# Gated linear attention feeding a softplus feed-forward layer: first four blocks loaded in pairs with two tokens per partition, loads strictly in turn, headwise score products, bias sum late

## The chip, the cores and the metric

The kernel runs on one core of one Trainium2 chip. The metric is the device time of one execution, in microseconds (us). A run of the unchanged kernel stands beside every run of a variant on the same chip. The kernel before takes 199.03 us (median of 3 runs, 198.89 to 200.34). A run is called slow when it is over 1.5% above the fastest run of the same kernel; comparisons use fast runs alone.

Five engines work side by side: TensorE (PE in the profile), VectorE (DVE), ScalarE (ACT), GpSimd (POOL) and SyncE (SP), which here issues all DMA transfers.

## The reference

```python
def _attn_ref(q, k, v, f_logit):          # each (4, 8, 768, 48)
    f = 1.0 / (1.0 + np.exp(-f_logit))
    state = np.zeros((B, H, D, D), dtype=np.float32)
    for t in range(S):
        state = f[:, :, t, :, None] * state + einsum('bhd,bhe->bhde', k[:, :, t], v[:, :, t])
        y[:, :, t] = einsum('bhd,bhde->bhe', q[:, :, t], state)
    return y
def _moe_ref(x, w_in, w_out):             # x (3072, 384), w_in (384, 2048), w_out (2048, 384)
    h = x @ w_in
    g = np.maximum(h, 0.0) + np.log1p(np.exp(-np.abs(h)))
    return g @ w_out
```

`x` is the attention output with the 8 heads of 48 side by side. The kernel works in 24 blocks of 128 tokens (4 batches of 6). In a block the running product of the gates becomes a prefix sum of logarithms, the in-block part a masked product of scores, and the earlier part a 48 x 48 state per head.

## The kernel before

A static list decides, ahead of time and from estimated costs, in which order each engine receives its tasks. A task names its engine, its cost, what it needs, a priority, and the buffers it takes and frees. So a change in one buffer count or cost can reorder every engine.

The loads: one 192 KB transfer for each of f, k, q and v of a block, in rows of one token of one head (48 floats, 192 bytes). The first four blocks go ahead of the eight weight quarters.

```python
def load(n, i):
    b, c = divmod(i, NC)
    t = work.tile([128, H, D], FP32, name=n + n, tag=n + n, bufs=LOADS)
    nc.sync.dma_start(
        out=t, in_=SRC[n][b, :, c * T:(c + 1) * T, :].rearrange("h p d -> p h d"))
    in_t[n, i] = t
# ... cut
turn = TURN or (blocks(0, 1, 2, 3) + [("wi", w) for w in range(4)]
                + [("wo", w) for w in range(4)])
```

The score products of blocks 4 to 23 take two heads at once, through a block-diagonal copy of q that costs VectorE two copies of 48 rows:

```python
def a_bd(i):
    pv, qbd = qkT_ps[i, 0], qbd_bufs[i % 2]
    nc.vector.tensor_copy(out=qbd[0:48, :, 0:128], in_=pv[0:48])
    nc.vector.tensor_copy(out=qbd[64:112, :, 128:256], in_=pv[64:112])
def a_p(i, half):                       # two calls of two matmuls for a block
    ps = att_bank("pp")
    for u in range(2):
        p = 2 * half + u
        nc.tensor.matmul(out=ps[:, u * 256:(u + 1) * 256], lhsT=qkT_t[i][0:112, NP + p, :],
                         rhs=qbd_bufs[i % 2][0:112, p, :], start=True, stop=True,
                         skip_group_check=True)
```

The softplus is computed as ln(0.5 e^h + 0.5), so the missing ln 2 comes back as a bias on the output, ln 2 times the column sums of w_out. GpSimd makes it with 15 additions, `sum`, from the staged weights; blocks finished earlier get it later through `add`:

```python
for n, (w, j) in enumerate(sums):
    task(("sum", n), "POOL", 0.91, [("at", "wo", w), ("sum", n - 1)], 40 + 3 * n, add_w, (w, j))
# ... cut
def store(i):
    nc.sync.dma_start(out=out[i * T:(i + 1) * T, :], in_=osb_t.pop(i))
    if i in (19, 20, 21):               # loads that nothing reads
        m = 2 << (i - 19)
        t = consts.tile([96, H, m, D], FP32, name=f"rows{m}")
        nc.sync.dma_start(out=t, in_=q[0, :, 0:96 * m, :].rearrange("h (p m) d -> p h m d", m=m))
```

The feed-forward layer is `f1` (48 matmuls of 128 columns for a block), two activations, and `f2` (16 matmuls of 384 columns).

## Time and profile before

| | before |
|---|---|
| time, median | 199.03 us |
| span of the profiled run | 197.0 us |
| first feed-forward matmul starts | 24.72 us |
| holes of TensorE after that | 6.7 us |
| last matmul starts, then the tail | 193.31 us, 3.66 us |
| VectorE, GpSimd busy | 142.9, 98.1 us |

The span is from the first to the last instruction of one profiled execution. A matmul's useful time is the distance from its start to the next start, capped at the median of its line; what exceeds that is a **hole**. Matmuls of fewer rows than the array are kept apart, with the excess ahead of their group (entry) and behind it (exit).

The page of the kernel before says, in its busy row and in the shares of the chain that ended last:

```profile
PE 184.4 (94%) x2491; PEld 152.7 (78%) x2491; DVE 142.9 (73%) x336; ACT 150.1 (76%) x251; POOL 98.1 (50%) x142
...
PE 57%; DVE 12%; SPq 10%; POOL 8%; DMA 6%; ACT 3%; issue 2%; ACTq 0%; POOLq 0%
```

The first line alone would say that TensorE is full at 94%, but 13.9 us of that are matmuls that only keep the clock up. In the chain TensorE has 57%; for the rest of the span the chain runs through other engines and transfers.

### The profile page before, as it was taken

Reading aid. Unit: us, or ns where it says so; the run is one execution under the profiler, and the core shown is the slowest. Engines: PE = TensorE matmul, PEld = TensorE weight load, DVE = VectorE, ACT = ScalarE, POOL = GpSimd, SP = SyncE. Lnnn points to the kernel's source line nnn. Section 1 sums busy time; section 2 is a strip of 40 time slices with the busy share of each in tenths; the row PEclk is TensorE's granted clock in tenths of the full one; section 3 lists DMA queues with packets and bytes.
Section 4 is the critical chain, followed back from the end, with each engine's and each line's share of the span. In section 5 each row is a group of like instructions: output and inputs, shape, how many; then the busy total and the mean of one; then the engine's idle time right before and its main releaser. Section 6 shows DMA issues by size and latency. Waiting matters only on the chain.

```text
span 197.0 us, 6209 instructions
## 1 busy us (share of the span) xinstructions
PE 184.4 (94%) x2491; PEld 152.7 (78%) x2491; DVE 142.9 (73%) x336; ACT 150.1 (76%) x251; POOL 98.1 (50%) x142
## 2 busy tenths in 40 slices
PE   6886997899999999989999999999999999999993
PEld 5775786666687888868888888888888888888872
DVE  6543774625999989999989889858778988773011
ACT  4566388886859996987989797898879778766770
POOL 2266867999997652652463364344246334500000
PEclk9999999999999999999999999999999999999998
DMA  6999999999999999999978757846541101102676
GB/s 124 188 189 176 352 382 374 244 198 187 188 165 194 186 190 173 277 195 208 233 146 172 144 118 160 161 113 137 113 90 41 42 2 43 40 29 75 163 188 171
DMA packets 109532, 32.34 MB, mean 164 GB/s; under 512 B 101184, under 2 KB 107968, under 8 KB 109504
## 3 DMA queue, kind: packets, MB, share of 16 engines
q1 hardware_dynamic: 109504, 31.96, 78.4%
q8 instruction: 19, 0.31, 0.7%
q14 instruction: 9, 0.07, 0.1%
HBM read 27.23 MB, written 4.72 MB: 162 GB/s over the span
## 4 chain that ended last, share of the span: by engine, by line
PE 57%; DVE 12%; SPq 10%; POOL 8%; DMA 6%; ACT 3%; issue 2%; ACTq 0%; POOLq 0%
PE hh L407 22%; PE ops L427 21%; SPq L140 8%; DMA w<-in_moe_w_out_dram 6%; POOL wsum L213 4%; PE qkT L268 3%; PE pp L303 3%; DVE ptm L315 3%; DVE ect L336 2%; POOL w_out_bf L191 2%; SPq L177 2%; PE oo L379 2%; DVE osb L458 1%; PE xTp L393 1%; PE ops L434 1%
## 5 line engine op out<-in xcount | busy, mean ns | idle before, releaser
L407 PE MATMUL hh<-xT,w_in_bf 128*128 128x128 bf16 x1152 | 112.3, 219 | 1.6 <-ACT uexp L415 0.9
L427 PE MATMUL ops<-w_out_bf,gg 128*128 128x384 bf16 x368 | 107.8, 326 | 1.0 <-POOL w_out_bf L191 0.9
L407 PEld LDWEIGHTS <-w_in_bf 128*128 128x128 bf16 x1152 | 88.0, 98 | 22.5 <-DVE xT L191 0.9
L415 ACT ACTIVATE uexp<-hh 128x512 f32<-128x512 f32 x96 | 56.5, 596 | 24.9 <-PE hh L407 24.1
L421 ACT ACTIVATE gg<-uexp 128x1024 bf16<-128x1024 f32 x48 | 50.7, 1056 | 1.4
L427 PEld LDWEIGHTS <-gg 128*128 128x128 bf16 x368 | 35.2, 98 | 5.3 <-issue 1.5
L363 POOL TENSOR_TENSOR sst<-tt,ect 48x192 bf16<-48x192 f32 x32 | 16.5, 517 | 31.7 <-DVE tt L354 25.5
L315 DVE TENSOR_TENSOR ptm<-pp,mask 128x512 bf16<-128x512 f32 x48 | 31.0, 684 | 1.6 <-PE pp L303 1.2
L250 POOL TENSOR_TENSOR qkp<-kk,ee 128x384 bf16<-128x384 f32 x23 | 21.1, 917 | 21.7 <-ACT ee L242 14.1
L191 DVE COPY qkT<-qkT 128x512 bf16<-128x512 bf16 x41 | 17.4, 423 | 13.8 <-PE qkT L268 9.6
L254 POOL TENSOR_TENSOR qkp<-qq,ee 128x384 bf16<-128x384 f32 x24 | 22.2, 924 | 0.3
L336 DVE STREAM_TRANSPOSE ect<-ee 32x128 bf16<-32x128 bf16 x64 | 19.5, 305 | 1.5
L191 POOL CAST vb<-vv 128x384 bf16<-128x384 f32 x24 | 12.6, 524 | 15.5 <-DMA vv<-in_v_dram 10.7
L229 ACT ACTIVATE ff<-ff 128x384 f32<-128x384 f32 x24 | 12.2, 516 | 7.0 <-DMA ff<-in_f_logit_dram 7.0
L454 DVE TENSOR_TENSOR osb<-ops,bias_bc 128x384 f32<-128x384 f32 x16 | 8.9, 556 | 9.4 <-PE ops L427 9.1
L618 PE MATMUL ops<-negU,ident 128*128 128x128 bf16 x169 | 13.9, 233 | 1.9 <-POOL ident masks.py:199 1.9
L213 POOL TENSOR_TENSOR wsum<-wsum,w 128x384 f32<-128x384 f32 x14 | 14.5, 1034 | 0.5
L191 DVE CAST xx<-oo 128x384 bf16<-128x384 f32 x21 | 11.7, 556 | 4.2 <-PE oo L379 3.9
L618 PEld LDWEIGHTS <-ident 128*128 128x128 bf16 x169 | 11.3, 105 | 4.4 <-issue 1.9
L242 ACT ACTIVATE ee<-cs 128x384 bf16<-128x384 f32 x24 | 11.5, 479 | 3.2 <-PE uu L323 1.7
L268 PE MATMUL qkT<-ident,qkp 128*128 128x128 bf16 x160 | 12.7, 219 | 1.0 <-POOL qkp L254 1.0
L303 PE MATMUL pp<-qbd,qkT 112*128 112x256 bf16 x80 | 12.9, 272 | 0.0
(60 smaller groups left out, 201.9 us busy)
## 6 DMA issues: line engine op xcount, KB each, us to landing
ff<-in_f_logit_dram SPq DMA_DIRECT2D x24, 192.0 KB, 4.5
kk<-in_k_dram SPq DMA_DIRECT2D x24, 192.0 KB, 4.4
qq<-in_q_dram SPq DMA_DIRECT2D x24, 192.0 KB, 4.2
vv<-in_v_dram SPq DMA_DIRECT2D x24, 192.0 KB, 4.4
out_dram<-osb SPq DMA_DIRECT2D x23, 192.0 KB, 2.4
w<-in_moe_w_in_dram SPq DMA_DIRECT2D x4, 768.0 KB, 8.6
w<-in_moe_w_out_dram SPq DMA_DIRECT2D x4, 768.0 KB, 12.7
rows<-in_q_dram SPq DMA_DIRECT2D x1, 1152.0 KB, 7.3
```

The lines of the kernel that those rows point to most:

```text
L191: on[eng].tensor_copy(out=out, in_=in_)
L213: nc.gpsimd.tensor_tensor(out=wsum, in0=wsum, in1=t[:, j, :], op=ALU.add)
L250: on[eng].tensor_tensor(out=qkp_bufs[i % 3][:, H:2 * H, 0:D], in0=in_t.pop(("k", i)), in1=e_bufs[i % 2][:, H:2 * H, 0:D], op=ALU.mult)
L254: on[eng].tensor_tensor(out=qkp_bufs[i % 3][:, 0:H, 0:D], in0=in_t.pop(("q", i)), in1=e_bufs[i % 2][:, 0:H, 0:D], op=ALU.mult)
L303: nc.tensor.matmul(out=ps[:, u * 256:(u + 1) * 256], lhsT=qkT_t[i][0:112, NP + p, :], rhs=qbd_bufs[i % 2][0:112, p, :], start=True, stop=True,
L315: nc.vector.tensor_tensor(out=to, in0=p_ps.pop((i, half)).rearrange("p (a t) -> p a t", t=128), in1=mask4, op=ALU.mult)
L336: nc.vector.transpose(out=t[32 * r:32 * r + 32], in_=e[96:128, 0:NP, 32 * r:32 * r + 32])
L407: nc.tensor.matmul(out=h_ps[i, j // 4][:, j % 4, :], lhsT=w_in_bf[:, r, j * 128:(j + 1) * 128], rhs=xT_t[i][:, r, :], start=(r == 0), stop ...
L415: nc.scalar.activation(out=u_t[i, a // 2][:, 4 * (a % 2):4 * (a % 2) + 4, :], in_=h_ps.pop((i, a)), func=AF.Exp, bias=0.0, scale=1.0)
L421: nc.scalar.activation(out=g_t[i][:, 8 * a:8 * a + 8, :], in_=u_t.pop((i, a)), func=AF.Ln, bias=0.5, scale=0.5)
L427: nc.tensor.matmul(out=o_ps[i][:, 0:DM], lhsT=g_t[i][:, j, :], rhs=w_out_bf[:, j, :], start=(j == 0), stop=(j == NJ - 1), skip_group_check ...
L618: nc.tensor.matmul(out=idle_ps[:, 0:128], lhsT=ident, rhs=negU, start=True, stop=True, skip_group_check=True)
```

## The change

The intent, in five parts:

1. Blocks 0 to 3 come as two pairs of 256 tokens. A partition holds two neighbouring tokens, so a row of a load has 384 bytes instead of 192, and 8 transfers replace 16. The attention of a pair is rewritten for interleaved tokens, with matmuls of 64-row tiles.
2. Transfers are issued strictly in turn (`before` below), with 5 instead of 8 weight staging buffers and 3 instead of 4 block buffers.
3. The score products of blocks 4 to 23 are made headwise, 8 matmuls of 48 rows from both halves of the array, so the block-diagonal copies go and one 1024-column copy replaces four.
4. The bias sums run late, and 13 instead of 7 blocks get their bias by an addition on GpSimd. There are 16 instead of 6 output buffers.
5. The loads that nothing reads, at the end, go.

Smaller edits ride along: other buffer counts in the attention, a set-up shared between VectorE and GpSimd, another number of matmuls that keep the clock up, and two stores instead of one for each paired block.

```diff
-SPREAD = 4
-HEADWISE = 4
+PAIRED = 4
-BIAS = 110
-LATE = 7
-LOADS = 4
+SUMS = 110
+BIAS = 240
+LATE = 13
+LOADS = 3
@@ load
+        if i < PAIRED:
+            t = work.tile([128, H, 2, D], FP32, name=n + "2", tag=n + "2", bufs=2)
+            nc.sync.dma_start(out=t, in_=SRC[n][b, :, c * T:(c + 2) * T, :].rearrange(
+                "h (p e) d -> p h e d", e=2))
+            in_t[n, i], in_t[n, i + 1] = t[:, :, 0, :], t[:, :, 1, :]
+            return
@@ pair attention (one of six new functions; the others are cut)
+    def a_p2(i, e, b):
+        lo = 64 * b
+        for p in range(NP):
+            for n in range(2):
+                nc.tensor.matmul(out=ps[64 * n:64 * n + 64, p, :],
+                                 lhsT=qkT_t[i, 1][lo:lo + 48, p, n, e, :],
+                                 rhs=qkT_t[i, 0][lo:lo + 48, p, n, :, :], start=True, stop=True,
+                                 skip_group_check=True)
@@ blocks 4 to 23
-    def a_bd(i):
-        ...
+    def a_ev(i, eng):
+        qkT_t[i] = work.tile([128, 2 * NP, 128], BF16, name="qkT", tag="qkT", bufs=2)
+        copy_on(eng, qkT_t[i], qkT_ps.pop(i))
@@ bias and stores
-        nc.vector.tensor_tensor(out=osb_t[i], in0=osb_t[i], in1=bias_bc, op=ALU.add)
+        nc.gpsimd.tensor_tensor(out=osb_t[i], in0=osb_t[i], in1=bias_bc, op=ALU.add)
-        if i in (19, 20, 21):
-            ... (the loads that nothing reads)
@@ order of transfers
+        before = ("go",) + turn[kd - 1] if kd else None
-            task(("go", n, i), "SP", 0.5, [(used[n], i - LOADS)], kd, load, (n, i))
+            task(("go", n, i), "SP", 0.55,
+                 [before, (used[n], i - LOADS) if i - LOADS >= PAIRED else None], kd, load,
+                 (n, i))
@@ sums
-        task(("sum", n), "POOL", 0.91, [("at", "wo", w), ("sum", n - 1)], 40 + 3 * n, add_w, (w, j))
+        task(("sum", n), "POOL", 1.08, [("at", "wo", w), ("sum", n - 1), ("xe", 4)], SUMS + 8 * n, add_w, (w, j))
```

## The prediction

> **What bounds the kernel now.** I read the page first, then the timeline of the first 42 us engine by engine, then the chain of waits, then busy time by stage.
>
> The page's time slices:
>
> ```profile
> PE   6886997899999999989999999999999999999993
> ...
> PEclk9999999999999999999999999999999999999998
> DMA  6999999999999999999978757846541101102676
> GB/s 124 188 189 176 352 382 374 244 198 187 188 165 194 186 190 173 277 195 208 233 146 172 144 118 160 161 113 137 113 90 41 42 2 43 40 29 75 163 188 171
> ```
>
> A slice is 4.9 us. TensorE (PE) looks busy from the start, but L618 (169 matmuls into a bank nobody reads) only keeps its clock up. DMA is saturated for the first 100 us, and moves about 188 GB/s with the 192-byte rows of q, k, v and f but 352 to 382 GB/s while the weights come (slices 5 to 7). The timeline shows when real feed-forward work begins:
>
> ```profile
> 16.41 0.34 PE L374 MATMUL oo<-sst,qkT 112*128 112x96 bf16 x4
> 16.58 0.36 PE L379 MATMUL oo<-vb,ptm 128*128 128x48 bf16 x8
> 18.39 0.32 PE L237 MATMUL cs<-zz,negU 128*128 128x384 bf16 x1 [1.45 <-ACT zz L233]
> ...
> 24.72 1.50 PE L407 MATMUL hh<-xT,w_in_bf 128*128 128x128 bf16 x24
> ...
> 23.29 1.01 POOL L191 CAST w_in_bf<-w 128x768 bf16<-128x768 f32 x1 [0.21 <-DMA w<-in_moe_w_in_dram]
> ```
>
> Block 0 has its x transposed by 14.2 us, yet the first feed-forward matmul (L407) starts at 24.72, when the casts of the first weight quarter, which the DMA released at 23.2, are done. So the start is bound by **16 small loads ahead of the weights in one queue**: the DMA records show 192 KB done every 1.05 us, the sixteenth at 19.05. The next stage, in the chain of waits:
>
> ```profile
> 20.54 11.15 DMA w<-in_moe_w_out_dram
> 31.74 1.22 POOL w_out_bf L191
> ...
> 43.25 1.00 POOL wsum L213
> 44.40 0.88 issue
> 45.28 0.92 POOL qkp L250
> 46.20 0.88 POOL qkp L254
> 47.13 0.40 PE qkT L268 x4
> ```
>
> After the last weight load GpSimd (POOL) spends 31.7 to 44.4 us on casts and bias sums, and only then makes block 4's k and q products. Busy time by stage:
>
> ```profile
> 24.00:44.00 20.00, 17.85 (x240) 14.33 (x238) 10.73 (x17) 16.10 (x26) 16.05 (x18) 1.00 1.06 303
> 44.00:64.00 20.00, 18.83 (x241) 14.74 (x240) 17.34 (x44) 15.32 (x28) 18.35 (x25) 1.00 1.24 184
> 64.00:90.00 26.00, 25.37 (x341) 21.06 (x340) 24.64 (x59) 22.79 (x40) 14.11 (x20) 1.00 1.09 205
> 90.00:190.00 100.00, 100.00 (x1350) 83.25 (x1349) 75.63 (x181) 82.01 (x134) 36.72 (x55) 1.00 0.50 110
> ```
>
> Columns: stage, length, then PE, weight load, VectorE (DVE), ScalarE (ACT), POOL, clock, DMA. From 90 us PE is full; in 64 to 90 DVE is nearly full too (24.6 of 26). Before that PE has holes.
>
> **My account of PE.** I took each matmul's start to the next start, capped at its group's median, as useful time: 167.1 us without L618. Of it 5.8 lies before 24.72. The holes after 24.72 sum to 7.0 us (3.1 up to 40, 2.2 in 40 to 60, 0.5 to 80, 1.0 in 80 to 100, 0.3 later). The last matmul starts at 193.3, then 3.7 us go to the last eviction and store. Check: 24.7 + 161.3 + 7.0 + 3.7 = 196.7, against 197.0. The first term and the holes are what a change can win; the measured time is 2.0 above the span (199.03 against 197.0).
>
> **What the Trainium skill says.** "DMA: Bandwidth & Descriptors", Specifications, puts the smallest transfer for line rate at 512 B. The trace agrees in direction: a packet of 192 B takes 16 ns in the median (12 B/ns), of 1536 B 66, of 2048 B 84 (24 B/ns); 384 B stays below that size. "TensorEngine Tiling (Array Packing)", Key Properties, says that tiles work independently, and that changing the tiling mode drains TensorE. The trace agrees with both: eight 48-row matmuls of both row halves start 28 ns apart, but start to the next ordinary matmul is 0.34 us, and four of one half alone need 0.33. "GPSIMD Engine Reference", Key points, warns that it shares SBUF interfaces with VectorE; the trace's wsum additions at 1034 ns against 555 for an addition on DVE fit a slower engine, and no record separates contention.
>
> **The change, part by part.**
>
> 1. Loads. Eight pair loads replace sixteen. A 384 B packet: between 16 ns at 192 B and 66 at 1536 B a line gives 23.4. 393,216 B are 1024 packets, 64 per engine: 1.5 us, against 2 x 1.05. Eight save 8 x 0.6 = 4.8 us of the queue ahead of the weights. First data flows at about 2.0 us (first 192 KB done at 2.95); so f done 3.5, k 5.0, q 6.5, v 8.0, second pair 9.5 to 14.0, first weight quarter (2.13 us each, from the records) 16.2. From data done to consumer the trace has 0.9 to 1.6 us: weights usable 17.6, cast (1.0) 18.6.
>
> 2. Pair attention must be ready then. f seen at 4.5; four activations at about 0.41 spacing and 0.52 long: 6.3; prefix sums (two accumulating 384-column matmuls per half, still at slow clock): 7.0; four exponentials: 8.6; products on POOL, 2 x 0.91: 10.3; transposes 0.4; eviction on ACT, 1024 columns, about 1.0, but its program order puts the second pair's first activations (f at 10.6) ahead: 12.4; four masks on DVE at 0.65 plus two state additions 0.73: 16.2; outputs, copy, transpose, copy: 18.4. So both inputs meet at 18.4 to 18.6. I take the first feed-forward matmul at **18.8**, a gain of 5.9. The two halves are balanced, so neither alone would give it.
>
> 3. PE work. A pair costs about 5.1 us (prefix sums 0.65, transposes 0.9, u 0.8 plus drains 0.2, products 0.9 with drain, o 1.3, x transposes 0.34) where two blocks before cost 3.4: +3.3 for both pairs, nearly all in the start. Headwise products in the other 20 blocks: 4 x 0.109 = 0.436 before; 0.34 plus an unknown entry drain (I guess 0.06) after, in 18 blocks where the order of instructions keeps all eight together; in two blocks they are split 4 and 4 (0.65): 18 x -0.04 + 2 x 0.21 = -0.3, call it -0.5. Before the first feed-forward matmul lies one pair plus the next one's prefix sums, 5.9. Remaining: 167.1 + 3.3 - 0.5 - 5.9 = 164.0.
>
> 4. Bias sums late, and 13 adds on POOL. The 15 sums (15.5 us) leave the path to block 4: its f lands after the last weight quarter (31.2 + 1.05 + 1.2 = 33.4), and the same steps as in the trace (two activations, sums, exponentials, products 1.85, eviction 0.8, masks 1.35, copies) put its x at about 43. PE has work till then: from 18.8 two pairs' f1 and four f2 (10.8 + 10.4) plus attention 6 is 27, to 46. The sums refill idle POOL time, 3.4 us used of 7 per block.
>
> 5. VectorE. Per block the two 48-row copies (0.41 + 0.43) and two 512-column evictions (0.42 each) become one 1024-column copy, about 0.8: 20 x 0.85 = 17 us less of 143, in the stretch where DVE was full. It removes the 0.8 us hole at 87 and most of the small ones; off the path after 90.
>
> 6. Removed read-only loads at the end, larger output buffers: nothing on the path.
>
> Holes left: while weight quarters come. POOL's order has a state product and both q products of pair two between the casts of quarters 0 and 1, so quarter 1 is usable at about 22.2 instead of 20.8: about 2 us of holes up to 30, 1 in 30 to 47, 1 after. I choose 4.0 against 7.0.
>
> Sum: 18.8 + 164.0 + 4.0 + 3.7 = 190.5 span; + 2.0 = 192.5. Leaning a little on the DVE relief, **192.2 us**, 3.4% faster.
>
> **Rivals.** (a) The longer pair chain, not the queue, sets the start: two tokens per partition delay the first block (before, x of block 0 was ready at 14.2; I compute 18.4). If ACT or DVE order adds 2 us, the time is 194.5. The static order makes this the likeliest miss. (b) The gain is given back: PE starts early but waits for weight quarters, which come at 2.13 us against 0.67 us of work per block and quarter. Then holes grow to 7 to 8: 196, "same". Against it: two blocks are ready together, so each quarter feeds 1.34 us plus pair two's attention. (c) TensorE mode switches cost more than 0.1 each: 0.2 more in 20 blocks is +4. Against it: the measured 0.34 includes the exit. (d) Full gain and DVE no longer slowing anything: holes 2, first matmul at 18: 189.5.
>
> **Range and chances.** Start +-1.2, holes -2/+3, drains +-1: range 189.0 to 196.0. Slower by over 2% (203) would need the start gain lost and drains on top: 0.02. Within 2% means over 195.05: 0.12. Faster: 0.86.
>
> **What would show it.** Right: pair loads done every 1.5 us; first L407-type matmul (feed-forward hidden) near 18.8, released by a weight cast or x copy; no long POOL run of wsum before block 4's products; DVE about 125 us busy; PE without holes from about 50. Wrong: 384 B packets over 28 ns; the start set by DVE masks or the ACT eviction after 20 us; gaps over 0.15 us on both sides of each product group in the steady stage; POOL state products waiting behind wsum sums.

## More of the kernel before

The changed kernel did not run beside the variants. These stand in other rounds, on three chips, where the kernel before had medians of 198.88 to 199.34 us. So differences of a few tenths of a us between a variant and the changed kernel need support from their profiles.

## The result

The changed kernel takes **193.39 us** (median of 4 runs, 193.34 to 193.56) against 199.06 us for the kernel before in the same rounds. The ratio is 0.971, with a 95% interval of 0.967 to 0.975: faster by 2.9%. A ratio, here and below, is the mean time of one kernel's fast runs over that of the other's fast runs of the same rounds, so it is not quite the ratio of the medians. The outputs are correct. The profiled span is 191.7 us.

First the time slices of the changed kernel's page (4.8 us each):

```profile
PE   6999889999999999999999999999999999999993
...
DMA  6999999999999963854655683687799910110112
GB/s 159 261 270 384 382 374 247 177 190 169 203 168 200 159 119 62 163 119 89 125 112 104 121 160 67 110 159 188 163 299 194 284 50 33 41 46 0 44 41 84
```

The second and third slices move 261 and 270 GB/s where before they moved 188 and 189: these are the 384-byte rows. The weights (382 to 384) begin one slice earlier. Now the timeline of the start, picked out of all engines:

```profile
4.45 0.94 ACT L249 ACTIVATE f<-f 128x384 f32<-128x384 f32 x2 [2.44 <-DMA f<-in_f_logit_dram]
...
10.48 0.94 ACT L249 ACTIVATE f<-f 128x384 f32<-128x384 f32 x2 [2.21 <-DMA f<-in_f_logit_dram]
11.32 1.00 ACT L209 ACTIVATE qkT<-qkT 128x1024 bf16<-128x1024 bf16 x1
...
18.11 0.69 DVE L211 CAST w_in_bf<-w 128x768 bf16<-128x768 f32 x1 [1.02 <-DMA w<-in_moe_w_in_dram]
...
18.40 0.94 ACT L209 ACTIVATE xT<-xTp 128x384 bf16<-128x384 bf16 x2
...
18.94 0.68 PE L474 MATMUL hh<-xT,w_in_bf 128*128 128x128 bf16 x9
```

The cast of the first weight quarter ends at 18.80 and the first x copy at about 18.9; the first feed-forward matmul follows at 18.94, 5.78 us earlier than before. The two inputs meet within 0.1 us. The eviction at 11.32 stands behind the second pair's first activations, which waited for their f until 10.48. Next, busy time by stage, in the columns that the prediction explains:

```profile
24.00:44.00 20.00, 19.38 (x283) 15.19 (x280) 13.19 (x24) 17.32 (x31) 10.91 (x17) 1.00 1.09 245
44.00:64.00 20.00, 20.00 (x294) 16.27 (x292) 15.27 (x36) 17.30 (x30) 18.21 (x25) 1.00 1.16 185
64.00:90.00 26.00, 26.00 (x373) 21.00 (x371) 18.71 (x42) 22.63 (x40) 19.06 (x26) 1.00 0.59 111
```

TensorE is full from 44 us on, and VectorE falls from 24.64 to 18.71 of 26 us between 64 and 90. In the changed kernel's chain, TensorE has 86% instead of 57%:

```profile
PE 86%; SPq 4%; DMA 4%; POOL 3%; DVE 1%; issue 1%; POOLq 0%
```

What TensorE's instruction starts add up to, in us:

| | before | predicted | after |
|---|---|---|---|
| start of the first feed-forward matmul | 24.72 | 18.8 | 18.94 |
| matmul work after it, with entries and exits | 161.9 | 164.0 | 166.7 |
| holes after it | 6.7 | 4.0 | 2.7 |
| tail from the last matmul's start | 3.66 | 3.7 | 3.32 |
| span | 197.0 | 190.5 | 191.7 |

So the start and the holes give 9.8 us, the tail 0.3, and 4.8 us of it goes to more work behind the first feed-forward matmul. Of that work 0.8 us is headwise products (worked out below); the rest was not split up. It should be mostly attention of the second pair, and mode switches (between matmuls on the whole array and on parts of it), that now lie behind the earlier start.

### The profile page after: what moved, and what is told of

The parts are those of the page before. It is cut to its first block, busy times and chain, and to the rows that moved or that the text cites. A ratio compares the mean times of both kernels' runs of the same rounds, so it can differ in the third digit from the quotient of the medians.

```text
span 191.7 us, 6346 instructions
## 1 busy us (share of the span) xinstructions
PE 184.8 (96%) x2613; PEld 150.4 (78%) x2613; DVE 126.6 (66%) x274; ACT 149.3 (78%) x249; POOL 108.5 (57%) x154
## 4 chain that ended last, share of the span: by engine, by line
PE 86%; SPq 4%; DMA 4%; POOL 3%; DVE 1%; issue 1%; POOLq 0%
PE hh L474 33%; PE ops L494 32%; PE qkT L296 5%; SPq L141 4%; DMA v<-in_v_dram 4%; PE pp L374 4%; PE oo L446 2%; PE xTp L460 2%; PE cs L257 2%; PE oo L441 2%; PE uu L391 1%; PE ops L501 1%; POOL qkp L282 1%; POOL sst L430 1%; POOL vb L211 1%
## 5 line engine op out<-in xcount | busy, mean ns | idle before, releaser
L383 DVE TENSOR_TENSOR ptm<-pp,mask 128x512 bf16<-128x512 f32 x40 | 25.8, 686 | 7.5 <-PE pp L374 7.4
L278 POOL TENSOR_TENSOR qkp<-kk,ee 128x384 bf16<-128x384 f32 x20 | 18.3, 915 | 20.6 <-ACT ee L270 9.1
L211 DVE COPY qkT<-qkT 128x1024 bf16<-128x1024 bf16 x22 | 15.2, 689 | 17.0 <-PE qkT L296 16.4
L282 POOL TENSOR_TENSOR qkp<-qq,ee 128x384 bf16<-128x384 f32 x20 | 18.4, 918 | 0.0
L525 POOL TENSOR_TENSOR osb<-osb,bias_bc 128x384 f32<-128x384 f32 x13 | 12.7, 1005 | 0.9 <-DVE bias_bc L243 0.9
L717 PE MATMUL ops<-negU,ident 128*128 128x128 bf16 x135 | 11.1, 244 | 1.9 <-POOL ident masks.py:199 1.9
L211 POOL CAST vb<-vv 128x384 bf16<-128x384 f32 x20 | 10.1, 507 | 4.5 <-DMA vv<-in_v_dram 4.5
L521 DVE TENSOR_TENSOR osb<-ops,bias_bc 128x384 f32<-128x384 f32 x10 | 5.6, 558 | 10.5 <-PE ops L494 10.3
L421 DVE TENSOR_TENSOR tt<-uu,sst 48x192 f32<-48x192 f32 x32 | 11.3, 354 | 0.9
L717 PEld LDWEIGHTS <-ident 128*128 128x128 bf16 x135 | 9.6, 112 | 2.3 <-POOL ident masks.py:199 1.9
```

Source lines behind the costliest of these rows:

```text
L211: on[eng].tensor_copy(out=out, in_=in_)
L278: on[eng].tensor_tensor(out=qkp_bufs[i % 4][:, H:2 * H, 0:D], in0=in_t.pop(("k", i)), in1=e_bufs[i % 2][:, H:2 * H, 0:D], op=ALU.mult)
L282: on[eng].tensor_tensor(out=qkp_bufs[i % 4][:, 0:H, 0:D], in0=in_t.pop(("q", i)), in1=e_bufs[i % 2][:, 0:H, 0:D], op=ALU.mult)
L383: nc.vector.tensor_tensor(out=ptm_t[i].rearrange("p (a b) t -> p b a t", b=2)[:, half, :, :], in0=p_ps.pop((i, half)).rearrange("p (a t) - ...
L717: nc.tensor.matmul(out=idle_ps[:, 0:128], lhsT=ident, rhs=negU, start=True, stop=True, skip_group_check=True)
```

## The experiments

Theory A, from the prediction: the larger rows set the start, headwise products cost TensorE nothing, the late bias frees GpSimd for block 4, and the loads that nothing reads are hidden. Rivals: the order of transfers sets the start; the bias sums no longer matter once TensorE has enough work; the mode switches of headwise products are on the path; the reads matter. Not tested alone are the loads in turn, on either kernel, and the smaller edits. All twelve variants gave correct outputs.

### 1. Row size alone

```diff
-            nc.sync.dma_start(out=t, in_=SRC[n][b, :, c * T:(c + 2) * T, :].rearrange(
-                "h (p e) d -> p h e d", e=2))
+            for e in range(2):
+                nc.sync.dma_start(out=t[:, :, e, :], in_=SRC[n][
+                    b, :, c * T + e:(c + 2) * T:2, :].rearrange("h p d -> p h d"))
```

This is the changed kernel with each pair load cut into two transfers of 192-byte rows. Every other engine has its instructions in the same order.

> The changed kernel with each pair load cut in two transfers, one per token parity, so that the rows are 192 bytes again; layout, arithmetic and the order of every engine are those of the changed kernel. Queue theory (row size sets the start): eight pair loads take about 2.1 us again instead of the 1.5 us seen, the first weight quarter comes 4.8 us later, the first feed-forward matmul moves from 18.9 to about 23.5 us and the time from 193.4 to about 197.9 us. Rival (the pair's own attention chain sets the start, the queue is hidden behind it): first feed-forward matmul at most 1 us later, 193.5 to 194.5 us.

Measured: 199.39 us (median of four runs, one of them slow; the three fast ones 197.75 to 200.28), ratio 0.997 (0.991 to 1.004). From the timeline of this variant:

```profile
23.94 0.69 DVE L212 CAST w_in_bf<-w 128x768 bf16<-128x768 f32 x1 [1.65 <-DMA w<-in_moe_w_in_dram]
...
24.29 0.94 ACT L210 ACTIVATE xT<-xTp 128x384 bf16<-128x384 bf16 x2
...
24.84 0.66 PE L475 MATMUL hh<-xT,w_in_bf 128*128 128x128 bf16 x9
```

The start is back at 24.84, 5.9 us later, and the fastest run is 4.4 us above the changed kernel's median. The cast of the weights moved by 5.83 us (18.11 to 23.94), and the x copy by 5.89. Both inputs of that matmul are late, so the rival (attention alone sets the start, and the queue is hidden) is out: the row size carries the start. The expectation put it at 23.5. Part of the difference lies in the loads: they cost the cast 5.83 us instead of 4.8. The sixteen cut loads, which read every other row, also let the first weight quarter be issued only at 17.62, against 16.87 after the sixteen whole ones of the kernel before. The rest is that attention is late too: the second pair's f comes later, the eviction of the first pair stands behind it on ScalarE, and TensorE has a hole of 3.6 us at 12.8; its granted clock is 0.51 from 13.8 to 20.7 us. So the time of this run contains some loss that is not the transfer itself.

### 2. No pairs

```diff
-PAIRED = 4
-LOADS = 3
+PAIRED = 0
+LOADS = 4
```

> The changed kernel with no block paired (first four blocks done as all others, 192-byte rows, four load buffers), bias sum late and headwise products kept. Queue theory: first feed-forward matmul near 24.5 us as before, but the holes after it are smaller than before (about 2.5 instead of 6.7 us) since the bias sums are off block 4's path, and the pairs' extra TensorE work is gone: about 195 to 196.5 us, so that pairing is worth 2 to 3 us of the 5.7. Rival (pairing is the whole gain): 198.5 to 199.5 us.

Measured: 197.00 us (196.34 to 197.08), ratio 0.988 (0.985 to 0.990); first feed-forward matmul at 24.31, holes 4.2 us. Pairing is worth 3.6 us (197.00 - 193.39), and all other parts together 2.0 to 2.3, by the rounds from which the kernel before is taken. It is less than the 5.4 us of start: without pairs the holes are 1.5 us larger, but TensorE has about 3 us less work behind its start (163.6 against 166.7). That fits more attention done before a later start, and dearer pairs (the prediction put a pair 1.7 us above two blocks); the two were not separated.

### 3. Headwise products on the kernel before

```diff
-HEADWISE = 4
-ON = {}
+HEADWISE = 24
+ON = {("evq", i): "DVE" for i in range(4, 24)}
```

> The kernel before with headwise products for all 24 blocks instead of four and nothing else. In the changed kernel's trace eight headwise matmuls with both mode switches cost TensorE 0.435 us against 0.437 us before, so TensorE gains nothing; VectorE loses about 17 us of copies. Theory: only the holes of 64 to 100 us (about 1.2 us) can go, and blocks whose eight are split cost 0.4 more: 198 to 199.5 us, same. Rival (VectorE, 24.6 of 26 us busy in that stage, was a bound): 196 to 197 us.

This is not quite part 3 of the change: here q and k are transposed into two banks and evicted by two copies, not by one of 1024 columns.

Measured: 202.25 us (median of four runs, one of them slow), ratio 1.011 (1.005 to 1.018). Neither theory had it slower. VectorE is relieved as intended, 142.9 to 127.3 us, but holes grow to 10 us. The profile was taken in the slow run, so it serves here for one mechanism and not for the size of the loss; the three fast runs, 200.39 to 203.14 us, scatter widely and all lie above the kernel before. The largest hole is in these lines of the variant's timeline, from SyncE's queue, ScalarE and TensorE:

```profile
88.14 2.37 SPq L461 DMA_DIRECT2D out_dram<-osb  x1
...
91.08 0.65 SPq L140 DMA_DIRECT2D ff<-in_f_logit_dram  x1
...
94.84 0.52 ACT L229 ACTIVATE ff<-ff 128x384 f32<-128x384 f32 x1 [3.71 <-DMA ff<-in_f_logit_dram]
...
95.90 0.33 PE L407 MATMUL hh<-xT,w_in_bf 128*128 128x128 bf16 x3 [2.23 <-ACT uexp L415]
```

A store held the queue from 88.14 for 2.4 us; the f load of a later block stood behind it and was issued at 91.08; ScalarE, whose order had the activation of that f ahead of the feed-forward's, stalled 3.71 us; TensorE waited for ScalarE. Relief of a busy engine did not become time, in fast runs either. What holds the fast runs back stays open: whether they have this same stall no profile shows, and I did not trace the other holes. So this run does not tell what headwise products are worth on the kernel before.

### 4. Late bias on the kernel before

The sums get priorities from 110 on and wait for block 4's x, the additions go to GpSimd, with 16 output buffers. To make room there are 6 weight staging buffers instead of 8, each freed after both of its casts (those lines are cut here).

```diff
-BIAS = 110
-LATE = 7
+BIAS = 240
+LATE = 13
-... name="w32", tag="w32", bufs=8)
+... name="w32", tag="w32", bufs=6)
-        task(("sum", n), "POOL", 0.91, [("at", "wo", w), ("sum", n - 1)], 40 + 3 * n, add_w, (w, j))
+        task(("sum", n), "POOL", 0.91, [("at", "wo", w), ("sum", n - 1), ("xe", 4)], 110 + 8 * n, add_w, (w, j))
```

> The kernel before with only the bias sum late (sums after block 4's input is made, 13 adds on GpSimd, 16 output buffers; for room six weight staging buffers instead of eight). Theory: the GpSimd run of sums leaves the path to block 4, holes between 40 and 65 us shrink from about 2.5 us by 1 to 2 us: 197 to 198 us. Rival (block 4 waits for its loads or VectorE anyway): 198.7 to 199.5 us.

Measured: 216.85 us (216.61 to 217.71), ratio 1.088 (1.085 to 1.092). The miss was of my own design. From the timeline of this variant, SyncE's queue and TensorE:

```profile
19.92 2.73 SPq L182 DMA_DIRECT2D w<-in_moe_w_out_dram  x2
22.77 2.91 SPq L140 DMA_DIRECT2D ff<-in_f_logit_dram  x1
...
47.49 1.41 SPq L182 DMA_DIRECT2D w<-in_moe_w_out_dram  x2
...
55.05 1.44 PE L427 MATMUL ops<-w_out_bf,gg 128*128 128x384 bf16 x4 [16.79 <-POOL w_out_bf L191]
```

Two of the four w_out loads were issued at 19.92, the other two only at 47.49: the list of this kernel let 16 block loads overtake them while no staging buffer was free. TensorE then waited 16.8 us for the cast. This shows what "strictly in turn" is there for: with fewer buffers, it keeps loads from overtaking those that are waited for.

### 5. Late bias on the kernel before, with loads in turn

The edits of experiment 4, and these:

```diff
+        before = ("go",) + turn[kd - 1] if kd else None
-            task(("go", n, i), "SP", 0.5, [(used[n], i - LOADS)], kd, load, (n, i))
+            task(("go", n, i), "SP", 0.5, [before, (used[n], i - LOADS)], kd, load, (n, i))
-            task(("go", n, i), "SP", 0.5, [], kd, load_w, (n, i), "w32",
+            task(("go", n, i), "SP", 0.5, [before], kd, load_w, (n, i), "w32",
```

> The late bias sum on the kernel before, as in the run that failed at 216.9 us, with one thing added: loads are issued strictly in turn, so that the last two output-weight quarters can no longer be overtaken by block loads while they wait for one of six staging buffers. If the overtaking was the whole 17 us hole, it goes: 197 to 199 us (late bias worth 0 to 2 us). If the late bias itself starves TensorE, well over 205 us again.

Measured: 197.02 us (196.97 to 197.07) against 198.88 in the same rounds, ratio 0.990 (0.988 to 0.993). Holes fall from 3.1 to 1.9 us before 45 us and from 3.3 to 2.2 between 45 and 100. So on the kernel before, the late bias and the loads in turn are together worth about 1.9 us, and the loss of the run above came from loads that overtook. What loads in turn alone would give was not run.

### 6. Early bias on the changed kernel

```diff
-SUMS = 110
-BIAS = 240
-LATE = 13
+SUMS = 40
+BIAS = 110
+LATE = 7
```

The additions also return to VectorE, and the sums no longer wait for block 4's x.

> The changed kernel with the bias sum early again (sums right after the last weights land, seven adds on VectorE), pairs and headwise products kept. Theory: the sums (15.5 us of GpSimd) delay block 4's products by several us, but TensorE has work till about 46 us by then, so 1 to 2.5 us of holes come back between 40 and 65 us: 194.5 to 196 us. Rival (bias placement is worth nothing, TensorE has enough other work): 193.2 to 193.8 us.

Measured: 194.02 us (193.88 to 194.07), ratio 0.973 (0.971 to 0.976). It is 0.6 us worse, or 0.35 if each is set against the kernel before of its own rounds: between what the two expectations allowed. After 30 us the holes are the same, 0.52 against 0.49 us; most of the difference is one product group more that was split in two (24 exits against 23). The holes side with the rival: once TensorE has the two pairs' feed-forward work to do, GpSimd's sums no longer delay what it needs next. What was worth 1.9 us on the kernel before, with loads in turn, is worth little here.

### 7. Block-diagonal products on the changed kernel

```diff
-    def a_p(i, b): ... 8 matmuls of 48 rows
+    def a_bd(i): ... two copies of 48 rows, as before
+    def a_p(i, half): ... 2 matmuls of 112 x 256, as before
-        osb = work.tile([128, DM], FP32, name="osb", tag="osb", bufs=16)
+        osb = work.tile([128, DM], FP32, name="osb", tag="osb", bufs=13)
```

> The changed kernel with the block-diagonal products of the kernel before in blocks 4 to 23 (two more 48-row copies, two evictions instead of one, 13 output buffers for room). Theory: TensorE spends 0.437 instead of 0.435 us per block, and 0.8 us less in the two blocks that were split; VectorE gets 17 us more (about 144 us) but with full TensorE queues from 30 us on hides most of it: 193 to 194.5 us, so the headwise products are worth about nothing here. Rival (VectorE's relief was what kept TensorE full): holes near 1.5 us or more come back at 60 to 100 us: 195 to 197 us.

Measured: two fast runs, 193.94 and 194.03, and two slow, 196.94 and 196.99; ratio of the fast ones 0.973 (0.970 to 0.977). In the fast runs headwise products are worth 0.5 to 0.6 us, or 0.3 against the kernel before of the same rounds. VectorE is at 144.0 us here against 126.6, and holes after 30 us are 1.9 instead of 0.5 us, which is where it shows, while TensorE's work after 30 us is 1.0 us less (156.9 against 157.9).

What a headwise group costs stands in TensorE's timeline of the changed kernel:

```profile
41.81 0.65 PE L494 MATMUL ops<-w_out_bf,gg 128*128 128x384 bf16 x3
42.39 0.41 PE L374 MATMUL pp<-qkT 48*128 48x128 bf16 x8
42.73 0.66 PE L494 MATMUL ops<-w_out_bf,gg 128*128 128x384 bf16 x3
```

Matmuls of 384 columns start 0.163 us apart, so the fourth was due at 42.30; the group begins at 42.39, 0.095 us late, and the next matmul starts 0.34 us after it. Together 0.435 us (the mean of 18 whole groups), against 0.437 to 0.439 us for the four block-diagonal matmuls of a block, which have no entry. TensorE saves nothing by headwise products, and the two blocks whose groups are split cost it 0.8 us in all. What is gained comes from VectorE.

### 8. All groups split

```diff
-                task(("p", i, b), "PE", 0.17, [("ev", i), ("p", i, b - 1)], s + 17 + b / 10,
+                task(("p", i, b), "PE", 0.17, [("ev", i), ("m", i, b - 1)], s + 17 + b / 10,
```

The second half of each product waits for the first half's mask, so each group of 8 becomes two of 4.

> The changed kernel with the two halves of each block's headwise products never issued together (the second waits for the first half's mask), so that each block of 4 to 23 pays both mode switches twice. Theory (TensorE is full, switches cost 0.095 us on entry and about 0.09 on exit): 18 more groups at 0.842 - 0.435 = 0.41 us: 7.3 us more, about 200.7 us. Rival (switches are hidden in waits): 193.4 to 195 us.

Measured: 201.04 us (200.94 to 201.22), ratio 1.009 (1.006 to 1.011), as expected to 0.4 us. Exits after 30 us rise from 23 to 41. A whole group costs 0.435 us and two of four cost 2 x 0.421, so 18 splits are 7.3 us by the instruction starts; the time rises by 7.65 us, and holes stay at 0.7. Mode switches in the full stage lie wholly on the path.

### 9. The unread loads put back

```diff
+        for m in {19: (2,), 20: (4,), 21: (4, 4)}.get(i, ()):
+            r = work.tile([128, 4, DM], FP32, name="w32", tag="w32", bufs=5)
+            r = r.rearrange("p j n -> p (j n)")[0:96, 0:m * DM]
+            nc.sync.dma_start(out=r.rearrange("p (h m d) -> p h m d", h=H, m=m),
+                              in_=q[0, :, 0:96 * m, :].rearrange("h (p m) d -> p h m d", m=m))
```

> The changed kernel with the three read-only loads of q behind the stores of blocks 19 to 21 put back (same sizes, into free weight buffers). In the traces the stretch from the last matmul to the end is 3.7 us before and 3.3 us after. Theory: they contend with the last stores, 0.2 to 0.4 us more: 193.6 to 193.8 us. Rival: no effect on any store: 193.3 to 193.5 us.

Measured: 194.99 us (194.42 to 195.13), ratio 0.978 (0.975 to 0.980). This is 1.3 to 1.6 us worse, more than either theory allowed. The profile is that of the fastest run, 194.42, whose span is 1.0 us longer: 0.7 us of it is in the tail, 4.01 against 3.32 us, and 0.2 in the start, which loads issued from 171 us on can't have moved. What the other three runs lose beyond it no profile shows. The tails of the other runs agree: 3.66 and 3.82 us with the loads (the kernel before and experiment 5), 3.23 to 3.32 without (experiment 2 and the changed kernel). The traces also say where the 0.7 us arises. The last two stores are issued in the same 1.65 us, and at the same distance from the last matmul, in both kernels, so it is not the queue's issue. But from issue to landing they take 2.9 us instead of 1.6 (median), and between 189 and 190 us the transfer engines have a busy share of 1.09 instead of 0.13: the stores' packets move among those of the loads.

### 10. The eviction first, and one cast on ScalarE

The changed kernel's remaining holes are 2.2 us before 30 us and 0.5 after. Two edits aim at the first: the second pair's activations wait for the eviction of the first pair's q, and one half of the second weight quarter is cast on ScalarE instead of GpSimd.

```diff
-ON = {}
+ON = {("cast", "wi", 1, 1): "ACT"}
-            task(("z1", i + e), "ACT", 0.52, [("f", i)], t - 6, z1, (i + e,))
+            task(("z1", i + e), "ACT", 0.52, [("f", i), ("ev", i - 2, 0)], t - 6, z1, (i + e,))
```

> An attempt to beat the changed kernel: ScalarE evicts the first pair's transposed q before it starts the second pair's activations (0.9 us earlier masks), and ScalarE casts half of the second weight quarter, which waited 2 us behind GpSimd's work. Theory (2.2 us of holes between 19 and 30 us and the start itself can shrink; one block fewer has its products split, 0.4 us): 192.2 to 193.0 us. Rival (the last input-weight quarter, usable at 26.7 us, sets the end of this stage whatever comes before): 193.0 to 193.6 us.

Measured: 192.64 us (192.54 to 192.70), ratio 0.968 (0.966 to 0.970), against 0.971 (0.967 to 0.975) for the changed kernel. The intervals overlap; the profile is what speaks for a gain: the holes before 30 us fell from 2.2 to 1.4 us, and one group fewer was split. But the start was not earlier (19.49). In this profile TensorE's clock opened 2 us later than in the changed kernel's, and VectorE's copy of the first pair's transposes began at 9.73 instead of 8.79, so that the eviction came only 0.09 us earlier (11.23). The clock is not shown to be the whole cause: in experiments 8 and 11 it opened almost as late (7.2 and 7.3 us against 7.7), and the start was at 19.15 and 19.07.

### 11. The eviction first, and the first weight quarter earlier

```diff
-            task(("z1", i + e), "ACT", 0.52, [("f", i)], t - 6, z1, (i + e,))
+            task(("z1", i + e), "ACT", 0.52, [("f", i), ("ev", i - 2, 0)], t - 6, z1, (i + e,))
+    turn.remove(("wi", 0))
+    turn.insert(turn.index(("v", 2)), ("wi", 0))
```

> As the run before in the eviction's place, but instead of the cast on ScalarE the first weight quarter is loaded ahead of the second pair's v, 1.5 us earlier. Theory (both inputs of the first feed-forward matmul move forward): first feed-forward matmul near 17.9 us instead of 18.9, one block fewer split, 192.0 to 193.0 us. Rival (the later quarters set the pace and the gain turns into holes before them): 193.0 to 193.6 us.

Measured: 193.62 us (193.49 to 193.81), ratio 0.973 (0.971 to 0.975), the same as the changed kernel within the intervals. The start did not move (19.07), and a hole of 1.5 us at 19.7 waits for GpSimd's q products of the second pair. Weights earlier than their x gain nothing.

### 12. The cast on ScalarE alone

```diff
-ON = {}
+ON = {("cast", "wi", 1, 1): "ACT"}
```

> The changed kernel with one half of the second weight quarter cast on ScalarE instead of GpSimd, and nothing else: the second part of the run that beat it at 192.64 us, without the earlier eviction. Theory A: the cast carries the gain, because GpSimd is then free 0.9 us earlier for the second pair's products and the later casts, so the hole before 30 us shrink from 2.2 us to about 1.5 and the time is 192.5 to 192.9. Theory B: the cast alone changes little (193.2 to 193.6) and the gain needs both parts, since the eviction on ScalarE decides when the second pair's activations run. In either case the feed-forward starts within 18.7 to 19.6 us.

Measured: **192.52 us** (192.44 to 192.61), ratio 0.967 (0.963 to 0.970): the fastest version measured, with one line. Its ratio's interval overlaps the changed kernel's (0.967 to 0.975), but the times of the two do not (193.34 to 193.56), and its holes agree. The time lies within Theory A: the cast carries the gain, and the eviction's order adds none that shows (192.64 with it, in other rounds). The timelines of the two kernels at the fourth weight quarter show how. First the changed kernel, with GpSimd's half of the cast, VectorE's half, and the matmul that waited:

```profile
25.34 0.83 POOL L211 CAST w_in_bf<-w 128x768 bf16<-128x768 f32 x1
...
25.50 1.22 DVE L211 CAST w_in_bf<-w 128x768 bf16<-128x768 f32 x1
...
26.77 0.34 PE L474 MATMUL hh<-xT,w_in_bf 128*128 128x128 bf16 x3 [0.59 <-DVE w_in_bf L211]
```

Then the timeline of the variant, in the same order:

```profile
24.59 0.83 POOL L211 CAST w_in_bf<-w 128x768 bf16<-128x768 f32 x1
...
25.54 0.68 DVE L211 CAST w_in_bf<-w 128x768 bf16<-128x768 f32 x1
...
26.30 1.00 PE L474 MATMUL hh<-xT,w_in_bf 128*128 128x128 bf16 x15 [0.25 <-ACT uexp L482]
```

GpSimd, spared one cast, finishes its half of the fourth quarter before VectorE begins the other half. VectorE's cast of the same 768 columns then takes 0.68 us instead of 1.22, and TensorE, which waited for it, goes on 0.47 us earlier; what it then waits for is an activation. The holes before 30 us fall from 2.2 to 1.6 us, and as the order shifts, one product group fewer is split. That the two casts hinder each other was not tested by itself, but the fourteen traces agree on it, and on who pays: the one that starts later. Where GpSimd's cast of a weight began 0.07 to 0.27 us before VectorE's and no other GpSimd work overlapped (8 times), it took 0.83 us and VectorE's 0.98 to 1.20; where VectorE's began up to 0.1 us before GpSimd's (40 times), it took 0.54 to 0.69 and GpSimd's 1.01 to 1.22.

### What each part is worth

By the differences of medians on the changed kernel: pairing 3.6 us (experiment 2), the removed loads 1.3 to 1.6 (9), headwise products 0.5 (7), late bias 0.6 or less (6). They sum to 6.0 to 6.3, against the 5.7 us between the two kernels; single removals need not add up exactly. Set against the kernel before of the same rounds, the four are 3.3, 1.3, 0.3 and 0.35 us. The last two are about as large as the shift between rounds, and the intervals of their ratios overlap the changed kernel's, so that they are above zero is not shown by the times alone.

## Why the prediction was right, and where its terms were off

The range and the mechanism held: 193.39 us against 192.2, within 189.0 to 196.0. The span was 191.7 against the sum of 190.5. The 2.0 us added to the span set a median of 199.03 against the span of a profiled run that took 198.75 itself; like for like it is 1.8, before and after.

- **Loads (part 1).** Right in its result: data of a pair load were done every 1.5 us, and experiment 1 shows that row size, not the number of blocks or the order, gives the start. The working by packet time was wrong: a 384-byte packet took 29 ns in the median, not the interpolated 23.4 (its own three figures give 23.1), and the prediction itself had named more than 28 as a sign of failure. The transfer still took 1.5 us, so packets of one engine overlap and a packet's recorded time is not its share of the transfer.
- **Pair attention (part 2).** Right step by step: f at 4.45 us (predicted 4.5), eviction done at 12.32 (12.4), masks done at 16.35 (16.2), first feed-forward matmul at 18.94 (18.8). On the weights' side two errors cancelled, which is luck: the cast began at 18.11 (17.6 predicted) and took 0.69 us instead of 1.0. The prefix sums did not run "still at slow clock": it opened at 5.6 us, before them. Rivals (a) and (b) did not occur.
- **TensorE work (part 3).** This is the term that was mis-sized: 164.0 predicted, 166.7 measured, 2.7 us. The step that failed is "0.34 plus an unknown entry drain (I guess 0.06)" and the "call it -0.5" built on it. The entry costs 0.095 us, and a group of 4 costs 0.421 us rather than half of 0.65. So 18 x 0.435 + 4 x 0.421 = 9.5 us stands against 20 x 0.437 = 8.7 before: +0.8 instead of -0.5, which explains 1.3 of the 2.7. Of the other 1.4, 0.6 is the coarser first sum (161.3 where the finer one finds 161.9). The rest may lie in the second pair, whose own switches up to 30 us measure 0.5 in entries and 0.7 in exits, where the prediction allowed little beyond 0.2 for a pair; I did not separate it. Rival (c) was the right worry, though a whole group's two sides, 0.095 and 0.092 us, stayed under the 0.15 that the prediction named as a sign of failure: experiment 8 shows each switch on the path.
- **Bias late (part 4).** The mechanism was right as far as block 4's k product now starts at 37.94 us instead of 45.28. But it was not needed: the prediction's own sum, work for TensorE until 46 us, says that a wait until 45 would have been hidden, and the holes of experiment 6 agree.
- **VectorE (part 5).** Right: 126.6 us busy (about 125 predicted), TensorE full from 44 us. The measured worth, 0.3 to 0.6 us, is small, as experiment 7 shows.
- **Removed loads (part 6).** "Nothing on the path" was wrong. Experiment 9 makes it 1.3 to 1.6 us, of which its profile shows 0.7 in the tail; the predicted tail of 3.7 us became 3.32.
- **Holes.** 2.7 instead of 4.0 us. The 2.2 before 30 us came as worked out ("about 2 us of holes up to 30"); the two further microseconds set aside for later shrank to 0.5.
- **Contention.** That "no record separates contention" is a misreading: in the kernel before, VectorE's cast of a weight took 0.69 us where it began first (at 23.19) and 1.14 where it began 0.24 us after GpSimd's (at 29.91), as in experiment 12. And the 555 ns set against GpSimd's additions belong to a copy; VectorE's additions took 556 where they read TensorE's results directly, and 631 where, like GpSimd's, they read staged copies.

The sum of the deviations is +0.1 (start), +2.7 (work), -1.3 (holes), -0.4 (tail): +1.1 of the 1.2 us in the span. So the near hit of the total is partly two errors of opposite sign. The final lean of 0.3 us toward relief of VectorE went the wrong way.

## What to carry to other kernels

When a queue of small rows stands ahead of the first real work, make the rows longer, but only as far as the other input of that work is ready at the same time; loading weights still earlier bought nothing. Count what a change adds on the full engine as carefully as what it removes elsewhere: groups that switch the array's tiling cost time on both sides, so keep them whole. Transfers that nothing waits for and engines that are "not the bound" can still cost time at the ends, and a part that helps one version of a kernel may be worth little on another, so measure it in place. When two engines slow each other's copies, look at which starts first: here the later one paid.

## What the Trainium skill lacked or had wrong

- "TensorEngine Tiling (Array Packing)", Key Properties, says that a change of mode drains TensorE but gives no cost. Here a group of 48-row matmuls among full ones cost 0.095 us on entry, and 0.148 us from its last matmul to the next instead of 0.056: about 0.19 us for each group.
- "DMA: Bandwidth & Descriptors" has a size for line rate but no rates below it for loads such as these. The slices here moved about 188 GB/s with rows of 192 bytes, 261 to 270 with 384, and 352 to 384 with the weights' rows. A packet's recorded time (29 ns for 384 bytes) did not predict the transfer's.
- "GPSIMD Engine Reference", Key points, says that GpSimd and VectorE share interfaces to SBUF, without durations. The sizes here, if this is the cause, for casts of 768 columns of w_in: VectorE's took 0.68 us alone and 0.69 when it began first, but 1.22 when it began 0.16 us after GpSimd's; GpSimd's took 0.83 when it began first and 1.08 when it began 0.03 us after VectorE's.
- "TensorE: Matmul & The Clock Gate", Part 1, puts the opening of the clock at around 4 us of sustained activity, within 500 ns (though it also calls the number of slow matmuls variable from run to run). Here matmuls of 128 columns went from 107 to 56 ns spacing between 4.5 and 7.7 us in thirteen profiles (all but the slow one), whose first matmul was always at 1.9: after 2.6 to 5.8 us. In two profiles of programs with the same first 43 matmuls, it was 5.66 and 7.68 us.
- No page tells what unread loads near the end cost the last stores: here the tail was 3.23 to 3.33 us without and 3.66 to 4.01 us with them, in profiles of fast runs.
